# The third gate/up piece is split into the sums' buffer, the first unit's h turns round in two parts, and split weights are stored later

## The chip, the core and the metric

One core of a Trainium2 chip runs the program. The metric is the device time of one execution in microseconds, the median of several runs; the program is the same in every run. The names of the engines are those of the profile: PE (TensorE, with PEld for its weight loads), DVE (VectorE), ACT (ScalarE), POOL (GpSimd) and SP (SyncE, which issues nearly all DMAs).

## What is computed

```python
xn = layernorm(x)                                   # x: 2048 x 576
q, k, v = split(xn @ wqkv)                          # 32 heads of 18
s = softmax(q @ k.T / sqrt(18)) @ v @ wo            # per head, 2048 x 2048 scores
g = silu(((xn @ w_gate) * (xn @ w_up)) @ w_down)    # w_gate, w_up: 576 x 4608
out = x + s * g
```

Both branches read the same normalised x. All inputs and the output are fp32.

## The kernel before, in words

**Precision.** A matmul operand of the projections and of the gated branch is split into a high part (a rounding copy by ACT) and a low part (value minus high part, by POOL), and the products high x high, low x high and high x low are summed in PSUM. "Splitting" a piece of weights below means these copies and differences.

**The gated branch** is cut into 72 units: 4 chunks of 512 rows (c) times 18 column blocks (q) of 256 columns. A unit has two *pieces* n = 2u and 2u+1, each 128 columns of w_up and w_gate together. Up columns stand on partitions 0 to 63 and gate columns on 64 to 127, so PE runs two streams side by side, each on one half of its rows: the *upper* stream does the "up" of a piece in 27 matmuls, the other its "gate" in 27 (L678). When an up is done, ACT copies its sum out (us, L683). When a gate is done, DVE multiplies the two (L690, h), ACT takes the high part (L693) and POOL the low part (L694), both into hs. The product with w_down (L720) needs h in both halves of the rows, so two DMAs carry hs crosswise into hx (the *turning round*, L710): one for each half of the rows, and the two streams then add hs and hx terms for four row blocks. The sums (acc) are gathered by DVE (L746, L748).

**The streams** run in this order: both pieces of unit u+1, then the down products of unit u. Beside them PE computes scores for the row maxima (pa, L596, reduced by DVE in L598), the scores again in transposed form (pb, L628, with exp by ACT in L630, two PSUM banks), and in *visits* of 28 matmuls (56 records of the trace) the products of the probabilities with v (L639).

**Weights in chunk 0.** A piece is loaded raw into wraw (two buffers, L116) and split into wgu, 128 x 18 x 128, two buffers: ACT's three copies in L193, POOL's three differences in L194. Piece n+2 goes into the buffer of piece n. The split piece is stored in DRAM as swg (L199, 1152 KB) so that chunks 1 to 3 can load it ready split (L185). w_down goes the same way through draw, wd and swd. `g_get` queues a piece's splitting as *chores*; `chore` runs one of them when the planner finds room.

**What sets the order.** Each engine runs its instructions in the order in which the code records them. A planner written in Python (`order`) keeps a clock for each of the two streams and a table of engines, PSUM banks and transfers with fixed costs, and records whatever can go next. So a changed cost or a changed call moves rows on all engines for the rest of the program. All of SP's DMAs stand in one queue, and an SP instruction that waits holds up the ones behind it.

**The buffer of the sums.** `accp` has one buffer, 128 x 4 x 576 of fp32. The sums of row chunks 0 and 2 live in it from the first down product of unit 0 on; before that it is unused.

Of the kernel before, what the change touches and what calls it, by code (L numbers as in the profile page):

```python
# [20 lines left out]
FT = mybir.dt.float32  # L21
# [19 lines left out]
def kernel(  # L41
# [10 lines left out]
    nc = tc.nc  # L52
# [109 lines left out]
    graw, gw, draw, dw = {}, {}, {}, {}  # L162
# [6 lines left out]
    def g_get(n):  # L169
# [13 lines left out]
        w = gw[n] = g_tile()  # L183
# [13 lines left out]
        def end():  # L197
            gdone.add(n)
            nc.sync.dma_start(swg[f], w.bitcast(FT))  # L199
            g_load(n + 2)  # L200

        chores.extend([(piece, (b,)) for b in (0, 3, 6)] + [(end, ())])

# [374 lines left out]
    with ExitStack() as mid:  # L578
# [106 lines left out]
        def gate_end(n, ps):  # L685
            u, j = divmod(n, 2)
            if j == 0:
                hs[u] = gp.tile([128, 2, 2, 512], FR, name="hs", bufs=2)
            h32 = us.pop(n)
            nc.vector.tensor_tensor(h32, ps, h32, op=OP.mult)  # L690
            g_get(n + 2)
            hj = hs[u][:, j]
            nc.scalar.activation(hj[:, 0, :], h32, AF.Copy)  # L693
            nc.gpsimd.tensor_tensor(hj[:, 1, :], h32, hj[:, 0, :].bitcast(FT), op=OP.subtract)  # L694
            if u == 0 and j or u == len(units) - 1:
                turn_round(u, j)
# [3 lines left out]
        def turn_round(u, j):  # L700

            if u == len(units) - 1:
                if j == 0:
                    hx[u] = accp.tile([128, 2, 2, 512], FR, name="hxl", tag="acc")
                js = slice(j, j + 1)
            else:
                hx[u] = gp.tile([128, 2, 2, 512], FR, name="hx", bufs=1)
                js = slice(0, 2)
            for r in range(2):
                nc.sync.dma_start(hx[u][half[r], js].bitcast(FT), hs[u][half[1 - r], js].bitcast(FT))  # L710
# [137 lines left out]
        def stream(r):  # L848

            for u in range(len(units) + 1):  # L850
                for n in (2 * u, 2 * u + 1):
# [4 lines left out]
                    for k in range(len(TERMS)):  # L856
                        def work(n=n, k=k, box=box, c=c, q=q):
                            if k == 0:
                                box.append(gu_start(r, n))
                            gu_op(r, n, box[0], k)  # L860
# [250 lines left out]
        def order():  # L1111
            nonlocal na, nb
            load_v(0)
            feeds = [stream(0), stream(1)]
            heads.extend(next(f) for f in feeds)
            wait = None
            while any(heads) or na < TOTAL or nb < TOTAL or due:
# [35 lines left out]
                elif op is not None:  # L1153
# [8 lines left out]
                    if end:  # L1162
# [11 lines left out]
                        else:  # L1174
# [20 lines left out]
        heads, stuck, parts, loaded, stacks = [], [False], {}, {}, []  # L1195
# [118 lines left out]
```

## Time and profile before

| | us |
|---|---|
| median of 3 runs (lowest, highest) | 2570.12 (2569.12, 2572.28) |
| the profiled execution, its time | 2571.43 |
| its span, first to last instruction | 2569.4 |
| PE busy | 2547.8 (99%) |
| ACT busy | 1467.1 (57%) |
| DVE busy | 1933.2 (75%) |
| DMA queue of SP, share of the 16 engines over the span | 68.6% |

PE's first matmul of the gated branch (L678) starts at 195.1 us, and its last matmul of the down products (L720) ends at 2501.1; between them is the *main phase*. PE is reported as busy when either half of it works, so a stretch in which only one stream runs still reads as 10 of 10 us busy; the number of matmuls in a stretch tells the difference. The granted clock is 1.00 in the windows shown below.

### The profile page before, as it was taken

How to read it: one execution, taken by the hardware profiler on the slowest of the kernel's cores; microseconds unless marked ns; L12 is line 12 of the kernel's file. 1: busy time of each engine (PE TensorE's matmuls, PEld its weight loads, DVE VectorE, ACT ScalarE, POOL GpSimd, SP SyncE). 2: the span in 40 equal slices, each digit the busy share in tenths (PEclk: the TensorE clock that was granted, in tenths of full speed). 3: DMA queues.
4: the chain of work that ended last, by engine and by line, in shares of the span. 5: the costliest groups of instructions: out<-in, count | busy, mean ns of one | idle time of the engine just before them, and what ended most of it. 6: DMA issues, size and time to landing. Idle time of an engine off the chain costs nothing.

```text
span 2569.4 us, 59203 instructions
## 1 busy us (share of the span) xinstructions
PE 2547.8 (99%) x24360; PEld 2111.1 (82%) x24360; DVE 1933.2 (75%) x3377; ACT 1467.1 (57%) x2688; POOL 594.8 (23%) x663
## 2 busy tenths in 40 slices
PE   8999999999999999999999999999999999999999
PEld 7899888878878888877888888777888877888878
DVE  6208778777778898777778888777888887778437
ACT  5222666666756665555665665555665655556651
POOL 3214434434421111111111111111111111111125
PEclk9999999999999999999999999999999999999999
DMA  7799988888886666665686656665686666654567
GB/s 243 235 284 278 263 226 225 232 225 220 221 206 186 176 182 177 175 179 155 179 197 173 179 175 184 176 170 154 179 204 166 180 184 176 175 174 146 159 189 248
DMA packets 195898, 504.58 MB, mean 196 GB/s; under 512 B 58112, under 2 KB 116352, under 8 KB 156588
## 3 DMA queue, kind: packets, MB, share of 16 engines
q1 hardware_dynamic: 185676, 489.05, 68.6%
q0 software_dynamic: 9952, 11.74, 1.7%
q8 instruction: 192, 3.15, 0.6%
q14 instruction: 78, 0.64, 0.1%
HBM read 312.21 MB, written 107.61 MB: 163 GB/s over the span
## 4 chain that ended last, share of the span: by engine, by line
PE 95%; DMA 3%; DVE 1%; SPq 0%; ACT 0%; issue 0%; POOL 0%; ACTq 0%; DVEq 0%
PE pg L678 34%; PE pg L639 18%; PE pg L720 16%; PE pa L596 12%; PE pb L628 8%; PE pg L402 2%; PE pa L348 2%; PE pb L348 2%; PE pg L1244 1%; DMA hx<-hs 1%; PE pb L1244 1%; PE pa L1244 1%; DMA sqk<-hl 0%; DMA ring<-sqk 0%; DMA xc<-sx 0%; DMA o<-sot 0%
## 5 line engine op out<-in xcount | busy, mean ns | idle before, releaser
L598 DVE TENSOR_REDUCE mx<-pa 128x1 f32<-128x512 f32 x2048 | 1367.1, 686 | 223.6 <-PE pa L596 104.8
L630 ACT ACTIVATE pt<-pb 128x512 f32<-128x512 f32 x2048 | 1161.9, 598 | 534.8 <-PE pb L628 465.5
L678 PE MATMUL pg<-xc,wgu 64*128 64x512 f32 x7776 | 1366.1, 388 | 0.7 <-DMA xc<-sx 0.5
L678 PEld LDWEIGHTS pg<-xc,wgu 64*128 64x128 f32 x7776 | 1051.7, 184 | 41.6 <-DMA xc<-sx 1.2
L628 PE MATMUL pb<-pair,ring 64*128 64x512 f32 x1997 | 777.4, 395 | 1.5 <-DMA ring<-sqk 1.5
L596 PE MATMUL pa<-pair,ring 64*128 64x512 f32 x2006 | 776.9, 393 | 1.8 <-DVE mx L598 1.8
L720 PE MATMUL pg<-wd,hs 64*128 64x288 f32 x3408 | 523.4, 292 | 0.0
L720 PE MATMUL pg<-wd,hx 64*128 64x288 f32 x3408 | 515.2, 292 | 2.4 <-DMA hx<-hs 2.4
L694 POOL TENSOR_TENSOR hs<-us,hs 128x512 fp32r<-128x512 f32 x144 | 186.2, 1293 | 1320.3 <-ACT hs L693 1285.6
L720 PEld LDWEIGHTS pg<-wd,hs 64*128 64x128 f32 x3408 | 459.8, 185 | 4.0 <-DVE acc L748 0.2
L720 PEld LDWEIGHTS pg<-wd,hx 64*128 64x128 f32 x3408 | 453.4, 185 | 6.5 <-DMA hx<-hs 3.0
L639 PE MATMUL pg<-pt,vt 128*32 128x512 f32 x4096 | 454.8, 594 | 0.7 <-DVE acc L748 0.6
L596 PEld LDWEIGHTS pa<-pair,ring 64*128 64x128 f32 x2006 | 364.3, 184 | 69.8 <-issue 52.8
L628 PEld LDWEIGHTS pb<-pair,ring 64*128 64x128 f32 x1997 | 362.5, 184 | 8.7 <-issue 1.9
L639 PEld LDWEIGHTS pg<-pt,vt 128*32 128x32 f32 x4096 | 125.5, 110 | 284.0 <-issue 278.9
L748 DVE TENSOR_TENSOR acc<-acc,pg 128x288 f32<-128x288 f32 x544 | 233.0, 443 | 22.4 <-PE pg L720 21.4
L645 DVE TENSOR_TENSOR oc<-oc,pg 128x512 f32<-128x512 f32 x69 | 47.1, 683 | 220.4 <-PE pg L639 213.7
L693 ACT ACTIVATE hs<-us 128x512 fp32r<-128x512 f32 x144 | 91.0, 632 | 151.0 <-DVE us L690 149.7
L194 POOL TENSOR_TENSOR wgu<-wraw,wgu 128x384 fp32r<-128x384 f32 x108 | 108.6, 1017 | 97.1 <-ACT wgu L193 84.6
L643 ACT ACTIVATE oc<-pg 128x512 f32<-128x512 f32 x32 | 19.2, 598 | 185.0 <-PE pg L639 179.0
L690 DVE TENSOR_TENSOR us<-pg,us 128x512 f32<-128x512 f32 x144 | 98.2, 682 | 26.9 <-PE pg L678 15.7
L618 POOL DMA_DIRECT2D pair<-mt x128 | 77.8, 613 | 166.4 <-DVE mt L613 162.3
(141 smaller groups left out, 1359.0 us busy)
## 6 DMA issues: line engine op xcount, KB each, us to landing
wgu<-swg SPq DMA_DIRECT2D x102, 1152.0 KB
hx<-hs SPq DMA_DIRECT2D x142, 512.0 KB
wd<-swd SPq DMA_DIRECT2D x50, 1152.0 KB
swg<-wgu SPq DMA_DIRECT2D x36, 1152.0 KB
pair<-sqk SPq DMA_DIRECT2D x192, 144.0 KB
ring<-sqk SPq DMA_DIRECT2D x384, 72.0 KB
swd<-wd SPq DMA_DIRECT2D x18, 1152.0 KB
sqk<-hl SPq DMA_DIRECT2D x32, 512.0 KB
```

The costliest lines, as they stand in the source:

```text
L194: nc.gpsimd.tensor_tensor(w[:, 9 + b:12 + b, :], raw[:, b:b + 3, :], w[:, b:b + 3, :].bitcast(FT), op=OP.subtract)
L348: nc.tensor.matmul(p, wq[b, a], xcs[c][:, e, :], start=n == 0, stop=n == len(PAIRS) - 1)
L596: nc.tensor.matmul(p, q[rows, t * 128:(t + 1) * 128], k[rows, c * 512:(c + 1) * 512], start=True, stop=True)
L598: nc.vector.tensor_reduce(mx[h][:, t, c:c + 1], p, axis=AX.X, op=OP.max)
L628: nc.tensor.matmul(p, k[rows, t * 128:(t + 1) * 128], q[rows, c * 512:(c + 1) * 512], start=True, stop=True)
L630: nc.scalar.activation(pt[t, c], p, AF.Exp, scale=scale)
L639: nc.tensor.matmul(p[32 * c:32 * c + 32, :], vt[h // 2][:, t, 6 * (h % 2):6 * (h % 2) + 32], pt[t, c], start=t == ts[0], stop=t == ts[-1])
L678: nc.tensor.matmul(ps, gw[n][half[r], a, :], xg[i][half[r], e, :], start=k == 0, stop=k == len(TERMS) - 1)
L690: nc.vector.tensor_tensor(h32, ps, h32, op=OP.mult)
L694: nc.gpsimd.tensor_tensor(hj[:, 1, :], h32, hj[:, 0, :].bitcast(FT), op=OP.subtract)
L720: nc.tensor.matmul(ps[:, 0:HALF], (hx if k else hs)[u][half[r], j, a, s * 128:(s + 1) * 128], dw[u][half[r], k, j, e, :], start=n == 0, st ...
L748: nc.vector.tensor_tensor(a, a, ps[:, 0:HALF], op=OP.add)
```

## The change

1. Piece 2 is split into a tile of the sums' buffer, called wg2, as soon as the planner starts, and not into piece 0's buffer after gate 0. The later pieces follow at other places: piece 3 takes piece 0's buffer after gate 0, piece 4 takes piece 1's after gate 1, gate 2 calls for nothing, and from gate 3 on piece n+2 follows gate n as before.
2. The store of a split piece to swg is taken out of the end of its splitting and goes where the gate stream starts on that piece. The next raw load, which stood behind the store, now stands alone.
3. Unit 0 turns its h round in two parts, one after each of its two gates, two DMAs of 256 KB each time.
4. The planner's table is told of the new places: when a piece counts as loaded, and 0.524 in place of 1.05 for unit 0's turning.

```diff
@@ -159,7 +159,7 @@
         c, q = units[u]
         return NF2 - 1 - q if c % 2 else q
 
-    graw, gw, draw, dw = {}, {}, {}, {}
+    graw, gw, draw, dw, unsaved = {}, {}, {}, {}, {}
     gdone, ddone = set(), set()
 
     def g_load(n):
@@ -180,7 +180,7 @@
             gw[n] = gw[n - 2]
             gdone.add(n)
             return
-        w = gw[n] = g_tile()
+        w = gw[n] = accp.tile([128, 18, 128], FR, name="wg2", tag="acc") if n == 2 else g_tile()
         if n >= 2 * NF2:
             nc.sync.dma_start(w.bitcast(FT), swg[f])
             gdone.add(n)
@@ -196,10 +196,18 @@
 
         def end():
             gdone.add(n)
+            unsaved[n] = f, w
+            g_load(n + 2)
+
+        chores.extend([(piece, (b,)) for b in (0, 3, 6)] + [(end, ())])
+
+    def g_save(n):
+        if n in unsaved:
+            f, w = unsaved.pop(n)
             nc.sync.dma_start(swg[f], w.bitcast(FT))
-            g_load(n + 2)
-
-        chores.extend([(piece, (b,)) for b in (0, 3, 6)] + [(end, ())])
+
+    def g_after(n):
+        return {0: 3, 1: 4, 2: None}.get(n, n + 2)
 
     def d_load(n):
         if n < NF2:
@@ -688,11 +696,12 @@
                 hs[u] = gp.tile([128, 2, 2, 512], FR, name="hs", bufs=2)
             h32 = us.pop(n)
             nc.vector.tensor_tensor(h32, ps, h32, op=OP.mult)
-            g_get(n + 2)
+            if g_after(n):
+                g_get(g_after(n))
             hj = hs[u][:, j]
             nc.scalar.activation(hj[:, 0, :], h32, AF.Copy)
             nc.gpsimd.tensor_tensor(hj[:, 1, :], h32, hj[:, 0, :].bitcast(FT), op=OP.subtract)
-            if u == 0 and j or u == len(units) - 1:
+            if u in (0, len(units) - 1):
                 turn_round(u, j)
 
         hx = {}
@@ -704,8 +713,9 @@
                     hx[u] = accp.tile([128, 2, 2, 512], FR, name="hxl", tag="acc")
                 js = slice(j, j + 1)
             else:
-                hx[u] = gp.tile([128, 2, 2, 512], FR, name="hx", bufs=1)
-                js = slice(0, 2)
+                if u or j == 0:
+                    hx[u] = gp.tile([128, 2, 2, 512], FR, name="hx", bufs=1)
+                js = slice(0, 2) if u else slice(j, j + 1)
             for r in range(2):
                 nc.sync.dma_start(hx[u][half[r], js].bitcast(FT), hs[u][half[1 - r], js].bitcast(FT))
 
@@ -857,6 +867,8 @@
                         def work(n=n, k=k, box=box, c=c, q=q):
                             if k == 0:
                                 box.append(gu_start(r, n))
+                                if r:
+                                    g_save(n)
                             gu_op(r, n, box[0], k)
                             if q == NF2 - 1 and n % 2 and k % 3 == 2 and c < NCH - 1:
                                 x_block(c + 1, k // 3, (64 * r,))
@@ -1111,6 +1123,7 @@
         def order():
             nonlocal na, nb
             load_v(0)
+            g_get(2)
             feeds = [stream(0), stream(1)]
             heads.extend(next(f) for f in feeds)
             wait = None
@@ -1175,11 +1188,12 @@
                             gated[n] = done
                             fin = engine("ACT", done + 0.05, 0.535)
                             fin = engine("POOL", fin + 0.05, 1.29)
-                            loaded[n] = moved(done - 0.4, 1.18) if (n // 2 + 1) % NF2 else 0.0
+                            if n != 2:
+                                loaded[g_after(n) - 2] = moved(done - 0.4, 1.18) if (n // 2 + 1) % NF2 else 0.0
                             if n // 2 == len(units) - 1:
                                 there["h", n // 2] = moved(fin, 0.524)
-                            elif n == 1:
-                                there["h", 0] = moved(fin, 1.05)
+                            elif n < 2:
+                                there["h", 0] = moved(fin, 0.524)
                             for _ in range(2):
                                 hot = n + 2 >= 2 * NF2 and n % (2 * NF2) in (34, 35, 0) and n + 2 < 2 * len(units)
                                 for want in stacks:
@@ -1192,7 +1206,7 @@
                 else:
                     clk[r] = max(clk[r] + 0.05, min(clk[1 - r] + 0.01, clk[r] + 0.3))
 
-        heads, stuck, parts, loaded, stacks = [], [False], {}, {}, []
+        heads, stuck, parts, loaded, stacks = [], [False], {}, {0: 0.0}, []
         order()
 
 
```

The built program's order shows it at three places.

SP's queue at the start of the main phase, before; `swg<-wgu` are stores of split pieces, `wraw` raw loads, the number behind a name its buffer (wgu_1762 is piece 1, wgu_2030 piece 2):

```order
112 L410 DMA sv_80<-vo2_427 128x608
113 L410 DMA sv_80<-vo0_423 128x608
114 L410 DMA sv_80<-vo4_1166 128x608
115 L410 DMA sv_80<-vo3_1164 128x608
116 L199 DMA swg_78<-wgu_1762 128x2304
117 L116 DMA wraw_1902<-in_B_w_up_dram 64x9x128
118 L116 DMA wraw_1902<-in_B_w_gate_dram 64x9x128
119 L584 DMA vt_1917<-sv_80 128x16x38
120 L199 DMA swg_78<-wgu_2030 128x2304
```

and with the change (wgu_1311 is piece 0, wraw_1900 the raw piece 3, wraw_1936 the raw piece 4):

```order
111 L418 DMA sv_80<-vo2_427 128x608
112 L418 DMA sv_80<-vo0_423 128x608
113 L418 DMA sv_80<-vo4_1166 128x608
114 L418 DMA sv_80<-vo3_1164 128x608
115 L116 DMA wraw_1900<-in_B_w_up_dram 64x9x128
116 L116 DMA wraw_1900<-in_B_w_gate_dram 64x9x128
117 L592 DMA vt_1915<-sv_80 128x16x38
118 L116 DMA wraw_1936<-in_B_w_up_dram 64x9x128
119 L116 DMA wraw_1936<-in_B_w_gate_dram 64x9x128
120 L207 DMA swg_78<-wgu_1311 128x2304
```

Piece 0's store, issued long before the main phase until now, stands behind two raw loads and the load of vt; piece 1's comes two rows later.

ACT with the semaphores that each row waits for (DMAHW are those of SP's DMAs), the copies out of up 0, up 1 and up 2 and the splits between them, before:

```order
118 L683 ACTIVATE us<-pg 128x512 [waits PE_49]
119 L693 ACTIVATE hs<-us 128x512 [waits DVE_49]
120 L193 ACTIVATE wgu<-wraw 128x384 [waits DMAHW5_49,PE_49,Pool_49]
121 L193 ACTIVATE wgu<-wraw 128x384 x2
122 L683 ACTIVATE us<-pg 128x512 [waits PE_49]
```

and with the change:

```order
121 L691 ACTIVATE us<-pg 128x512 [waits PE_49]
122 L702 ACTIVATE hs<-us 128x512 [waits DVE_49]
123 L193 ACTIVATE wgu<-wraw 128x384 [waits DMAHW4_49,DMAHW0_49,DMAHW7_49,PE_49,Pool_49]
124 L193 ACTIVATE wgu<-wraw 128x384 x2
125 L691 ACTIVATE us<-pg 128x512 [waits PE_49]
```

The split after gate 0, of piece 2 before and of piece 3 now, waits for three DMAs: the two raw loads of piece 3, and the store of piece 0 that reads the buffer which the split overwrites.

SP's queue in a later unit of chunk 0 (unit 5, pieces 10 and 11), before:

```order
164 L116 DMA wraw_3680<-in_B_w_up_dram 64x9x128
165 L116 DMA wraw_3680<-in_B_w_gate_dram 64x9x128
166 L710 DMA hx_3755<-hs_3381 64x2048 x2
167 L232 DMA swd_79<-wd_3754 128x2304
168 L124 DMA draw_3790<-in_B_w_down_dram 64x2x288 x4
169 L245 DMA ring_1154<-sqk_76 18x1024 x6
170 L245 DMA pair1_1153<-sqk_76 18x2048 x3
171 L199 DMA swg_78<-wgu_3905 128x2304
```

and with the change:

```order
163 L116 DMA wraw_3679<-in_B_w_up_dram 64x9x128
164 L116 DMA wraw_3679<-in_B_w_gate_dram 64x9x128
165 L720 DMA hx_3746<-hs_3368 64x2048 x2
166 L207 DMA swg_78<-wgu_3370 128x2304
167 L240 DMA swd_79<-wd_3745 128x2304
168 L124 DMA draw_3779<-in_B_w_down_dram 64x2x288 x4
169 L253 DMA ring_1154<-sqk_76 18x1024 x6
170 L207 DMA swg_78<-wgu_3547 128x2304
```

The store of the unit's first piece (wgu_3370) now stands right behind the turning of h, and that of the second (wgu_3547) behind the store of w_down's block, four raw loads of the next one and the ring's loads.

More of the change, by code (lines that the diff above doesn't have):

```diff
@@ L198, in end @@
             gdone.add(n)
-            nc.sync.dma_start(swg[f], w.bitcast(FT))
+            unsaved[n] = f, w
             g_load(n + 2)
         chores.extend([(piece, (b,)) for b in (0, 3, 6)] + [(end, ())])
+    def g_save(n):
+        if n in unsaved:
+            f, w = unsaved.pop(n)
+            nc.sync.dma_start(swg[f], w.bitcast(FT))
+    def g_after(n):
+        return {0: 3, 1: 4, 2: None}.get(n, n + 2)
     def d_load(n):
```

## The prediction

> **What bounds the kernel now.** I read the page's chain of waits first, then who waits for whom in chunk 0 (330 to 700 us), then the windows and the timelines of ACT and SP at the start of the main phase. The page's chain and the groups of the two ACT steps that matter here:
>
> ```profile
> PE 95%; DMA 3%; DVE 1%; SPq 0%; ACT 0%; issue 0%; POOL 0%; ACTq 0%; DVEq 0%
> L630 ACT ACTIVATE pt<-pb 128x512 f32<-128x512 f32 x2048 | 1161.9, 598 | 534.8 <-PE pb L628 465.5
> ```
>
> PE's waits from 330 to 700 us (row: who, for whom, us in total, times, longest), and from all groups the row of the splits:
>
> ```profile
> PE pg L678 <- DVE acc L748: 0.2, 1, 0.2
> ...
> PEld pa L596 <- DVE oc L645: 0.8, 1, 0.8
> ```
>
> ```profile
> L193 ACT ACTIVATE wgu<-wraw 128x384 fp32r<-128x384 f32 x108 | 54.1, 520 | 2.0 <-DMA wraw<-in_B_w_gate_dram 2.0
> ```
>
> PE sets the end. In chunk 0 it waits for almost nothing, and ACT stands still before all 108 split copies for 2.0 us together. What can be won lies at the start, and it is little; what can be lost is a PE that never waits now. The windows (us, busy and count by engine, clock, DMA share, GB/s):
>
> ```profile
> 200.00:210.00 10.00, 10.00 (x85) 9.55 (x82) 8.90 (x14) 3.07 (x6) 3.54 (x4) 1.00 1.03 328
> 210.00:220.00 10.00, 10.00 (x72) 8.14 (x71) 8.78 (x14) 2.52 (x5) 4.89 (x5) 1.00 1.17 224
> 270.00:280.00 10.00, 7.57 (x81) 6.85 (x79) 6.04 (x10) 5.01 (x10) 3.45 (x4) 1.00 0.98 249
> 380.00:390.00 10.00, 10.00 (x95) 10.00 (x94) 8.44 (x18) 7.72 (x14) 2.87 (x2) 1.00 1.03 247
> ```
>
> From 210 to 220 us only 72 matmuls run where 85 ran before: one half of PE is empty for a while. From 270 to 280 PE is idle for 2.43 us. The DMA engines are full (share about 1.0) in all four.
>
> **The change, part by part.** *Piece 2 earlier.* ACT's timeline around pieces 0 to 3 (start, duration, what), with POOL's part of a split:
>
> ```profile
> 201.52 0.60 ACT L683 ACTIVATE us<-pg 128x512 f32<-128x512 f32 x1 [5.92 <-PE pg L678]
> 205.75 0.63 ACT L693 ACTIVATE hs<-us 128x512 fp32r<-128x512 f32 x1 [3.63 <-DVE us L690]
> 206.29 1.34 ACT L193 ACTIVATE wgu<-wraw 128x384 fp32r<-128x384 f32 x3
> 208.80 0.60 ACT L683 ACTIVATE us<-pg 128x512 f32<-128x512 f32 x1 [1.18 <-PE pg L678]
> ...
> 218.72 0.60 ACT L683 ACTIVATE us<-pg 128x512 f32<-128x512 f32 x1 [3.20 <-PE pg L678]
> ```
>
> ```profile
> 207.72 2.96 POOL L194 TENSOR_TENSOR wgu<-wraw,wgu 128x384 fp32r<-128x384 f32 x3
> ```
>
> ```profile
> 195.09 0.49 PE L678 MATMUL pg<-xc,wgu 64*128 64x512 f32 x1
> ...
> 204.06 0.91 PE pg L678 x8
> ```
>
> The phase begins at 195.1. Eight matmuls of two streams take 0.91 us, so a stream needs 0.228 us for each and 6.2 us for the 27 of an up. Up 1 ends at about 208.4, up 2 at 218.3, so up 2 began near 212.1, 17.0 us into the phase. In the order before, the upper stream has 60 matmuls ahead of it (13.7 us); in the new order it has 59 (13.5 us) and no gap. Gain: 17.0 - 13.5, about 3.4 us. The split itself, 1.34 us of ACT and 2.96 of POOL, moves to where ACT is idle for 5.92 us and costs nothing; without that cover it would delay the first us copy by at most 1.3.
>
> *Stores later.* Piece n+2 overwrites piece n's buffer, so its split must wait until the store of piece n has landed. Until now that store was issued at least a gate earlier; now it is issued when gate n begins, and ACT, which runs in order, stands at the split until the DMA is through. Queued behind it on ACT are the copy of the next up and the exps, which give PE its banks back. The price is the landing time of the store against the length of a gate.
>
> SP's rows at the start, and the only turnings whose landing the chain of waits shows:
>
> ```profile
> 199.08 2.50 SPq L410 DMA_DIRECT2D sv<-vo  x4
> 207.57 0.38 SPq L584 DMA_DIRECT2D vt<-sv  x1
> 202.94 0.66 SPq L116 DMA_DIRECT2D wraw<-in_B_w_up_dram  x1
> 203.65 1.37 SPq L116 DMA_DIRECT2D wraw<-in_B_w_gate_dram  x1
> ```
>
> ```profile
> 239.12 8.29 DMA hx<-hs
> 266.87 11.50 DMA hx<-hs
> ```
>
> *The first store.* In the new queue piece 0's store follows the load of vt, which waits for the stores of sv and cannot go before 207.6, and a raw load of 0.66 + 1.37 us: it goes at 209.7. Two DMAs of this time landed 8.29 and 11.50 us after their issue with the queue as full as here; alone, 1152 KB (1.18 MB) at the 247 GB/s of 380 to 390 us take 4.8 us. Taking 8.3, it lands at 218.0. ACT reaches the split of piece 3 at 206.3 as before, and waits. Piece 3 is ready one copy (0.52) and POOL's 2.96 later, at 221.5. The new order has 91 matmuls ahead of up 3 on the upper stream, 20.8 us, so PE wants it at 195.1 + 20.8 = 215.9 and waits 5.6 us. With the gain: **+2.2 us** for the start; with 4.8 us of landing -1.3, with 11.5 +5.4.
>
> *A unit of chunk 0.* A gate takes 27 matmuls and, by the new order, 8 to 13 scores of its own half: 36 x 0.228 = 8.2 us. DVE's product and ACT's high part follow (these two groups, DVE and ACT):
>
> ```profile
> L690 DVE TENSOR_TENSOR us<-pg,us 128x512 f32<-128x512 f32 x144 | 98.2, 682 | 26.9 <-PE pg L678 15.7 <-PE pb L628 10.4
> L693 ACT ACTIVATE hs<-us 128x512 fp32r<-128x512 f32 x144 | 91.0, 632 | 151.0 <-DVE us L690 149.7 <-DMA hx<-hs 0.6 <-DMA ring<-sqk 0.6
> ```
>
> With 0.5 for the hand-overs, ACT asks for the buffer 10.0 us after the gate began, or 16.1 when a visit falls inside the gate:
>
> ```profile
> 299.36 6.15 PE pg L639 x56
> 329.49 6.14 PE pg L639 x56
> ```
>
> The first piece's store stands right behind the turning, which is issued about when its gate begins. With the 8.29 us row it lands at 8.3 + 4.8 = 13.1, so ACT stands still for 3.1 us; if the queue were empty, (1.05 + 1.18) MB at 247 GB/s give 9.0 and no wait. The second piece's store has the first one, swd, four raw blocks and itself behind that: 1.18 + 0.59 + 1.18 MB and some ring loads, 3.17 MB, 12.8 us later, at 21.8 to 25.9. Its gate begins 8.2 us after the first, so it lands 13.6 to 17.7 us into it: 3.6 to 7.7 us too late without a visit, 0 to 1.6 with one.
>
> PE feels a standing ACT only when both exp banks are full: one exp per 1.13 us (2048 in the phase of 2306 us) and two banks, so I let 1.5 us of each stall go free (between one exp, 0.6, and two intervals, 2.3). By the new order the visit lies in the second gate in units 4 to 8, in the first in units 9 to 13, in neither in 1 to 3 and 14 to 17. So the first piece stalls PE for 0 to 1.6 us in 12 units, 0 to 19; the second, in the four last without a visit, for 2.1 to about 4.6 us (the first stall has pushed the gate back by 1.6), 8 to 18; with a visit hardly. Which end is nearer, the later windows tell:
>
> ```profile
> 340.00:350.00 10.00, 10.00 (x127) 9.92 (x125) 10.00 (x20) 8.35 (x17) 3.06 (x3) 1.00 0.40 94
> 350.00:360.00 10.00, 10.00 (x92) 9.96 (x89) 8.95 (x15) 7.82 (x16) 4.93 (x5) 1.00 0.91 241
> ...
> 410.00:420.00 10.00, 10.00 (x102) 9.96 (x100) 9.08 (x17) 8.64 (x17) 5.80 (x5) 1.00 0.68 150
> ```
>
> The queue is neither empty there nor always as full as at 240, so I take the middle: **+9.6 and +13 us**. In units 1 to 3 no exps wait yet; left to the range.
>
> *The end of chunk 0.* Chunk 1's x blocks are loaded there and gate PE:
>
> ```profile
> 736.55 8.06 DMA xc<-sx
> 744.63 11.52 DMA ring<-sqk
> ```
>
> Piece 35's store now stands among them, ahead of 17 of the 20 loads: 0 to 4.8 us, taken as **+2.4**.
>
> *The turning of unit 0* in halves moves the same bytes with two more DMA issues; the second part goes after gate 1 as the whole did, so what the down products wait for last is half as large and no later: nothing. *The planner's new costs* reshuffle the rest, with the same number of matmuls. Laid out on the two halves at their durations, without any wait, the whole new order is 1.5 us shorter than the old one, less than the 3.4 of its start, so I count nothing more; chunks 1 to 3 have no stores of pieces.
>
> Sum: 2.2 + 9.6 + 13 + 2.4 = **+27.2 us**. The profiled span of 2569.4 becomes 2596.6; its execution's time was 2.0 above the span, and the median lies 1.3 below that time, so the median goes from 2570.1 to **2597.3 us**. The bounds add up to -1.3 + 0 + 8 + 0 = +7 and 5.4 + 19 + 18 + 4.8 = +47, 2577 to 2617: the forecast's own range.
>
> **Rivals.** *The stores land in time.* If a turning and a store behind it take less than the 10.0 us of a gate, ACT never stands, and the gain of 3.4 us stays, with up to 2.4 more if the turning behind PE's idle 2.43 us (270 to 280) comes sooner because no store waits for POOL ahead of it: 2564.3 to 2566.7. For it speaks that ACT waits 2.0 us in all today; against it the 8.29 and 11.50 us rows, which leave no room for 1.18 MB more. By the Trainium skill, "DMA: Bandwidth & Descriptors", section "Anatomy of one DMA — SWDGE (gpsimd) path", a DMA takes 2.0 us and its bytes at 436 GB/s; worked out from that, an estimate, turning and store need 7.1 us and the second store 7.3 more, and neither would be late. The windows' 224 to 328 GB/s at a share of 1.0 disagree with that rate here. Chance 0.14.
>
> *Only the start pays.* Once the queue has caught up, the exp banks swallow what is left of the stalls: +2.2, 2572.3. For it: 1.5 of 3.1 us are free already. Against: the second piece's store is late even with an empty queue. Chance 0.14.
>
> *The queue stays as full as at 267 us.* Each store lands 11.50 + 4.8 = 16.3 us after the turning, the first piece costs 4.8 us of PE in 12 units: 57 and more, 2630. This decides if later stores also hold the raw loads and turnings behind them back. The windows from 340 to 420 us do not look so full. Chance 0.08.
>
> **Chances and range.** The forecast has 0.64, the rivals 0.14, 0.14 and 0.08. A change under 0.2% (5.1 us) is about what cannot be told from none here. Faster by more: half of the first rival and a little, 0.08. Within: the rest of it and most of the second, 0.16. Slower: 0.76. The range 2567 to 2622 leaves out about half of the first rival and the third.
>
> **What would show it.** Piece 2: the second and third us copies of the upper stream 6 to 7 us apart. The stores: L193's idle time must rise from 2.0 to some 50 us or more, with the store swg<-wgu as releaser; PE's waits for the exps (pb, L630) must appear in chunk 0 and be absent in chunks 1 to 3; POOL's differences shift with ACT. If L193 still waits for some 2 us, the forecast falls whatever the time is. If the idle time is there but PE does not wait, the free 1.5 us was too little. If PE waits for other things (the sums' buffer, the ring), the place was wrong.

## The result and the profile after

| | before | after |
|---|---|---|
| median of 4 runs each, us (lowest, highest) | 2570.04 (2569.12, 2572.28) | 2610.07 (2605.55, 2612.99) |
| the profiled execution, its time | 2571.43 | 2605.55 |
| its span | 2569.4 | 2603.6 |

The ratio is 1.0147, with a 95% interval of 1.0135 to 1.0159: the change makes the kernel slower by 35 to 41 us (38 at the ratio). The forecast was slower, 2597.3, in a range of 2567 to 2622. The profiled execution of after is the fastest of its four runs, 4.5 us below their median; that of before lay 1.4 above. So the two traces differ by 34.1 us and the medians by 40.0.

The chain of waits of after by engine, the group of the split copies, and PE's waits from 195 to 800 us (who, for whom, us in total, times, longest):

```profile
PE 89%; DMA 5%; DVE 2%; SPq 1%; issue 1%; POOL 1%; ACT 1%; ACTq 0%; POOLq 0%; DVEq 0%
```

```profile
L193 ACT ACTIVATE wgu<-wraw 128x384 fp32r<-128x384 f32 x105 | 53.5, 522 | 45.9 <-DMA swg<-wgu 31.5 <-issue 6.7 <-DMA ring<-sqk 4.5
```

```profile
PE pb L636 <- ACT pt L638: 14.5, 8, 3.4
PE pb L636 <- DMA pair<-mt: 4.9, 1, 4.9
PE pa L604 <- DVE mx L606: 4.5, 1, 4.5
PE pg L686 <- DMA xc<-sx: 1.6, 2, 1.3
```

PE's share of the chain fell from 95 to 89%. ACT stood still ahead of the split copies for 45.9 us instead of 2.0, mostly until a store of a split piece (swg<-wgu) had landed. PE now waits for the exps (pt) in chunk 0, eight times and 14.5 us in all. From 800 to 2400 us it waits for none of them again; the largest row of PE there is this one:

```profile
PE pa L604 <- DVE mx L606: 1.5, 3, 0.5
```

One stall in full, in unit 6: the store on the chain from 365 to 390 us, then ACT's timeline, then PE's wait in the same window.

```profile
370.38 9.95 DMA swg<-wgu
```

```profile
376.03 1.07 ACT L638 ACTIVATE pt<-pb 128x512 f32<-128x512 f32 x2
380.43 0.52 ACT L193 ACTIVATE wgu<-wraw 128x384 fp32r<-128x384 f32 x1 [3.34 <-DMA swg<-wgu]
380.86 0.58 ACT L638 ACTIVATE pt<-pb 128x512 f32<-128x512 f32 x1
```

```profile
PE pb L636 <- ACT pt L638: 2.3, 1, 2.3
```

The store is issued at 370.38 and lands at 380.33. ACT has done its last exp at 377.1, stands before the split for 3.34 us, and the next exp starts at 380.86. Of the 3.34 us, PE loses 2.3.

Where the 34 us are lost is seen from the start of each up (its first matmul on PE, counted in the program's order from the first matmul of the phase; worked out from PE's records of both traces):

```
up                   2     3     4     6     8    10    12    16    26    28    32    36    40   end of phase
before, us        16.7  24.6  38.4  61.9  88.7 119.7 151.6 215.6 376.0 407.9 478.4 542.7 609.3
after - before    -3.2  +2.5  +3.8  +4.7  +9.8 +15.2 +17.0 +20.0 +19.8 +20.9 +25.8 +29.5 +31.5  +34.0
```

Unit u begins with up 2u. Units 2 to 7 lose 16 us, units 8 to 13 no more than 1, units 14 to 17 some 9, the turn to chunk 1 another 2.

Not all of the 34 us are waits. From 190 to 810 us PE stands idle for 26.6 us, 21.2 more than before. A second part is the granted clock. In the main phase of before it is 1.00 throughout; in the trace of after it falls to 0.50 in five stretches, one of 6.8 us from 216.7 and four of 3.4 us from 267.9, 312.3, 660.5 and 776.5. The window of the first one (us, busy and count by engine, clock, DMA share, GB/s), and the same kind of matmul in it and behind it:

```profile
210.00:220.00 10.00, 5.55 (x44) 4.66 (x42) 4.59 (x7) 2.66 (x6) 4.14 (x4) 0.84 0.92 312
```

```profile
222.02 0.62 PE L686 MATMUL pg<-xc,wgu 64*128 64x512 f32 x1
225.06 0.39 PE L686 MATMUL pg<-xc,wgu 64*128 64x512 f32 x1
```

PE works for 18.6 us of these 20.5 at half the clock, which costs some 9 us (an estimate: half of 18.6). Each stretch begins within a wait of PE or at most 1.5 us behind one. The four waits of 2.7 us and more (2.75 to 4.91) were all followed by one, and so was the turn to chunk 1, where the longest of several short waits is 1.35; two waits of 2.3 us, at 379 and 714, were not, and neither was that of 2.2 in before. That the waits bring the lower clock is read from this order in time; no run here changes the clock alone.

### The profile page after: what moved, and what is told of

It reads as the page before. It is cut to its first block, busy times and chain, and to the rows that moved or that the text cites. A ratio compares the mean times of both kernels' runs of the same rounds, so it can differ in the third digit from the quotient of the medians.

```text
span 2603.6 us, 59193 instructions
## 1 busy us (share of the span) xinstructions
PE 2559.3 (98%) x24360; PEld 2117.1 (81%) x24360; DVE 1930.9 (74%) x3377; ACT 1461.8 (56%) x2688; POOL 592.9 (23%) x663
## 4 chain that ended last, share of the span: by engine, by line
PE 89%; DMA 5%; DVE 2%; SPq 1%; issue 1%; POOL 1%; ACT 1%; ACTq 0%; POOLq 0%; DVEq 0%
PE pg L686 31%; PE pg L647 17%; PE pg L730 14%; PE pa L604 10%; PE pb L636 8%; DMA swg<-wgu 3%; PE pg L410 2%; PE pa L356 2%; PE pb L356 2%; PE pg L1258 1%; DVE mx L606 1%; DMA o<-sot 1%; PE pa L1258 1%; PE pb L1258 1%; DMA sqk<-hl 0%
## 5 line engine op out<-in xcount | busy, mean ns | idle before, releaser
L636 PE MATMUL pb<-pair,ring 64*128 64x512 f32 x2013 | 785.5, 396 | 19.6 <-ACT pt L638 14.5
L730 PE MATMUL pg<-wd,hx 64*128 64x288 f32 x3408 | 509.4, 292 | 0.0
L698 DVE TENSOR_TENSOR us<-pg,us 128x512 f32<-128x512 f32 x144 | 98.4, 684 | 24.7 <-PE pg L686 14.1
```

The lines of the kernel that those rows point to most:

```text
L636: nc.tensor.matmul(p, k[rows, t * 128:(t + 1) * 128], q[rows, c * 512:(c + 1) * 512], start=True, stop=True)
L730: nc.tensor.matmul(ps[:, 0:HALF], (hx if k else hs)[u][half[r], j, a, s * 128:(s + 1) * 128], dw[u][half[r], k, j, e, :], start=n == 0, st ...
```

## The experiments

Each experiment is timed against the kernel before on the same chip. Three theories go in. *Standing ACT*: the late store of the buffer's earlier piece holds the next split, and ACT, in order, holds the exps and us copies behind it. *New order*: the order of TensorE's work, the halved turning and piece 2's place cost the time. *Traffic*: late stores only crowd the DMA queue, and others wait for that. (A ratio's interval is given behind it; where two runs are compared by their ratios, both intervals count.)

**Stores early again, all else as changed.**

```diff
         def end():
             gdone.add(n)
-            unsaved[n] = f, w
+            nc.sync.dma_start(swg[f], w.bitcast(FT))
             g_load(n + 2)
```

> The change with its third part undone: the stores of split weights go at the end of the split again; piece 2 in the sums' buffer, the halved turning and the new order of the tensor engine stay. Standing ACT (a late store of a buffer's earlier piece holds the next split, and ACT stands in order before it): 2566 to 2572 us, idle time before the split copies (L193) back to 2 to 5 us. New order (the order, the halves or piece 2 cost the time, the place of the stores nothing): 2600 to 2610 us. Traffic (late stores collide in the DMA queue with turnings, ring and x loads, and PE waits for those): as standing ACT, 2566 to 2572 us.

Measured: 2580.85 against 2571.48, ratio 1.0039 (1.0025 to 1.0053). So 28 of the 38 us come with the late stores, but 10 do not, and neither figure expected held. PE's waits from 195 to 800 us in this run:

```profile
PE pb L636 <- DMA pair<-mt: 5.4, 1, 5.4
PE pa L604 <- DVE mx L606: 2.9, 1, 2.9
PE pg L730 <- DMA hx<-hs: 1.7, 1, 1.7
```

The waits for exps are all but gone (0.2 us); three others stay, and all come before 290 us. They are taken up below. The splits still stand for 11.9 us, more than the 2 to 5 expected, now with a raw load as releaser (wraw<-in_B_w_gate_dram). The clock is at 0.50 for 10.2 us, which is up to half of what stays.

**The late stores alone, in the kernel before.** The four places of the store as in the change, nothing else; TensorE's order is that of before.

```diff
         def end():
             gdone.add(n)
-            nc.sync.dma_start(swg[f], w.bitcast(FT))
+            unsaved[n] = f, w
             g_load(n + 2)
...
                             if k == 0:
                                 box.append(gu_start(r, n))
+                                if r:
+                                    g_save(n)
```

> The kernel before with the late stores alone: the store of piece n goes when gate n begins, everything else and the order of the tensor engine as before. Standing ACT: 2592 to 2606 us, the split copies' idle time 35 to 60 us with the store swg<-wgu as what ended it. New order: 2568 to 2572 us. Traffic: 2592 to 2606 us too, but with PE waiting for loads and turnings, not for the exps and the row maxima.

Measured: 2603.63, ratio 1.0119 (1.0104 to 1.0134), +31 us. The group of splits, PE's waits from 195 to 800 us, and the longest stall on ACT's timeline:

```profile
L193 ACT ACTIVATE wgu<-wraw 128x384 fp32r<-128x384 f32 x108 | 54.2, 520 | 50.7 <-DMA swg<-wgu 31.0 <-issue 12.3 <-PE pg L683 5.6
```

```profile
PE pb L633 <- ACT pt L635: 18.7, 5, 9.7
```

```profile
284.23 1.35 ACT L193 ACTIVATE wgu<-wraw 128x384 fp32r<-128x384 f32 x3 [11.62 <-DMA swg<-wgu]
```

The late stores make the loss by themselves, with the old order too, and PE waits for the exps above all: 18.7 us, against 4.4 for loads (xc, pair and ring). The longest stretch at half the clock, 13.7 us, begins within the longest wait, of 9.7 us.

**The same late traffic, but no split that waits for it.** The stores of pieces 0 to 33 read the x tile. Chunks 1 to 3 then load pieces 34 and 35 over and over (a second edit, not shown), so this kernel does not compute the formula; the DMAs are as many and as large.

```diff
     def g_save(n):
         if n in unsaved:
             f, w = unsaved.pop(n)
-            nc.sync.dma_start(swg[f], w.bitcast(FT))
+            if n < 34:
+                src = xg[0].rearrange("p a b -> p (a b)")[:, 0:2304]
+                nc.sync.dma_start(swg[f].rearrange("p a b -> p (a b)"), src.bitcast(FT))
+            else:
+                nc.sync.dma_start(swg[f], w.bitcast(FT))
```

> The change, but the late stores of pieces 0 to 33 read as many bytes from the x tile in place of the split weights, at the same place in the queue, so that no split has to wait for one; in chunks 1 to 3 the reloads take pieces 34 and 35 over and over. The number and size of all DMAs are the same; what chunks 1 to 3 compute is not the reference's. Standing ACT: 2566 to 2575 us, the split copies' idle time below 8 us. Traffic: 2598 to 2612 us, as the change, since every byte still moves late. New order: 2600 to 2610 us.

Measured: 2577.36, ratio 1.0021 (1.0011 to 1.0031). That is 2.4 us above what *standing ACT* had said and far below *traffic*. The split copies:

```profile
L193 ACT ACTIVATE wgu<-wraw 128x384 fp32r<-128x384 f32 x105 | 53.4, 522 | 3.4 <-DMA wraw<-in_B_w_gate_dram 3.4
```

The bytes of the late stores, at the same place in the queue, cost nothing that can be seen: this run is no slower than the one with early stores. What costs is that the split must wait for them. *Traffic* falls. *New order* falls as the main cause, but holds for the 5 to 10 us that stay.

**Half of each store late.** The high half of a piece is stored at the end of the split, the low half when the gate begins.

```diff
+            nc.sync.dma_start(swg[f][:, 0:9, :], w[:, 0:9, :].bitcast(FT))
             unsaved[n] = f, w
...
-            nc.sync.dma_start(swg[f], w.bitcast(FT))
+            nc.sync.dma_start(swg[f][:, 9:18, :], w[:, 9:18, :].bitcast(FT))
```

> The change, with the high halves of a piece (columns 0 to 8) stored at the end of the split and only the low halves when the gate begins: half the bytes are late. Standing ACT: the late half lands 2 to 3 us sooner, and what stands before the three copies is shorter by that in each unit, so less than half of the loss is left: 2576 to 2590 us, idle time before the copies 10 to 30 us. Traffic: half the late bytes, half the loss, about 2588 us or more. New order: 2600 to 2610 us.

Measured: 2587.77, ratio 1.0059 (1.0044 to 1.0074). Against early stores, half of the bytes late cost some 5 us (1.0059 less 1.0039; by the intervals 0 to 10) where all of them cost 28. The time fits both bounds, 2576 to 2590 for *standing ACT* and about 2588 for *traffic*, and decides nothing alone.

```profile
L193 ACT ACTIVATE wgu<-wraw 128x384 fp32r<-128x384 f32 x105 | 53.4, 522 | 23.1 <-DMA swg<-wgu 22.9
```

The idle time halves, and PE's waits for exps fall to a fifth (from 14.5 to 2.9 us): a stall of ACT costs PE only what is left after its banks' slack.

**Late only in units 8 to 13.**

```diff
-            unsaved[n] = f, w
+            if 16 <= n < 28:
+                unsaved[n] = f, w
+            else:
+                nc.sync.dma_start(swg[f], w.bitcast(FT))
```

> The change with the late stores in units 8 to 13 alone, where the visit lies in the first gate; in all other units the stores go at the end of the split. If a late store costs only where no visit covers its landing (the trace of the change grows by 15 us in units 2 to 7, by nothing in 8 to 13, by 9 in 14 to 17): as with all stores early, 2578 to 2584 us. If every late store costs alike (29 us over 17 units): 2588 to 2594 us.

Measured: 2583.31, ratio 1.0048 (1.0034 to 1.0062), against 1.0039 with all stores early. So these twelve late stores cost some 2 us together, which cannot be told from nothing; PE still waits for exps three times, 3.3 us in all. (In unit 8 the visit still lies in the second gate; from unit 9 on it lies in the first.) No group row names a store any more:

```profile
L193 ACT ACTIVATE wgu<-wraw 128x384 fp32r<-128x384 f32 x105 | 53.4, 522 | 17.4 <-PE pg L689 7.9 <-PE pa L607 4.4 <-issue 3.7
```

**Each store one gate earlier.**

```diff
                                 if r:
                                     g_save(n)
+                                    g_save(n + 1)
```

> The change with each late store issued one gate earlier (piece n+1 is stored when gate n begins; at the start piece 0 and 1 together). If the loss is the landing time of a store against the length of a gate: one gate more, 8 us or above, covers most landings, 2581 to 2587 us and less than 10 us of idle time at the splits with a store as what ended it. If stores anywhere behind the split cost (order of the queue, traffic): 2595 us or more.

Measured: 2595.40, ratio 1.0091 (1.0078 to 1.0105): half of the loss by the late stores is left. 2581 to 2587 us had been expected, and the time lies in the range that had been set for *traffic*; since the run with the x tile rules that out, the cause must be looked for in when the stores are issued. SP's timeline around the start of unit 4, first of the change, then of this run:

```profile
296.56 1.22 SPq L720 DMA_DIRECT2D hx<-hs  x2
...
300.01 5.61 SPq L207 DMA_DIRECT2D swg<-wgu  x1
...
313.41 0.34 SPq L207 DMA_DIRECT2D swg<-wgu  x1
```

```profile
290.31 1.22 SPq L720 DMA_DIRECT2D hx<-hs  x2
...
292.71 7.72 SPq L207 DMA_DIRECT2D swg<-wgu  x2
```

The odd piece's store, 13.4 us behind the even one in the change, now stands next to it. The even one hardly moves: it still stands behind the turning (hx<-hs) on SP, 2.4 us in place of 3.4. The idle time at the splits falls from 45.9 to 25.9 us, and PE's waits for exps from 14.5 to 9.5. This fits a price of landing time against the time until the split, but the place in the program did not give the time of issue; SP's order did.

**What stays with early stores: piece 2, the halves, the order.** Two runs start from the kernel before and do one part alone, with the old order of TensorE. A third does both.

```diff
-        w = gw[n] = g_tile()
+        w = gw[n] = accp.tile([128, 18, 128], FR, name="wg2", tag="acc") if n == 2 else g_tile()
...
-            g_get(n + 2)
+            if g_after(n):
+                g_get(g_after(n))
...
             load_v(0)
+            g_get(2)
```

> The kernel before with piece 2 split early into the sums' buffer, and nothing else: the turning whole, the stores at the end of a split, and the very order of TensorE's instructions as before (the planner's costs are left as they were). In the run with early stores 9 us of loss stayed, 3.3 of them behind up 2, where piece 3's raw block landed at 213.2 us behind the store of piece 1. If the new order and the halved turning make the rest: up 2 begins 3 us sooner, up 3 as before, 2568 to 2574 us. If piece 2's own place makes the loss (its buffer, its store, the raw blocks behind it): 2577 to 2583 us.

Measured for piece 2 alone: 2575.87, ratio 1.0019 (1.0010 to 1.0028), about 5 us slower (2.6 to 7.2). That lies between the two ranges expected, so neither held.

```diff
-            if u == 0 and j or u == len(units) - 1:
+            if u in (0, len(units) - 1):
...
-                hx[u] = gp.tile([128, 2, 2, 512], FR, name="hx", bufs=1)
-                js = slice(0, 2)
+                if u or j == 0:
+                    hx[u] = gp.tile([128, 2, 2, 512], FR, name="hx", bufs=1)
+                js = slice(0, 2) if u else slice(j, j + 1)
```

> The kernel before with the first unit's turning in two parts, and nothing else (order of TensorE's instructions as before). If the second part lands no later than the whole did: 2568 to 2573 us. If the halves cost the 3.4 us that the run with early stores lost between up 3 and up 4, where a half turning landed 10.7 us after its issue: 2573 to 2576 us.

Measured for the halves alone: 2571.27, ratio 1.0005 (0.9995 to 1.0014): nothing that can be told from zero.

Both together, with the old order (the two diffs above in one kernel):

> The kernel before with piece 2 early and the halved turning, stores at the end of the split, and the old order of TensorE's instructions: the run with early stores (2580.9) but for the order. If the new order costs what piece 2 alone (2575.9) and the halves alone (2571.3) leave over, some 4.5 us, most of it PE's wait for the first head's row pair (pair<-mt, landed 9.1 us after its issue): 2574 to 2578 us. If it is the two edits together and the order is innocent: 2579 to 2583 us.

Measured: 2575.65, ratio 1.0015 (1.0005 to 1.0024). With the new order the same edits had given 1.0039, so the new order costs about 6 us (2 to 11). Its sign in the trace is the wait for pair<-mt, the row maxima of the first head on their way into the pair tile: 5.4 us with the new order, and not among PE's waits in this run with the old one:

```profile
PE pa L604 <- DVE mx L606: 4.1, 2, 3.4
PE pg L730 <- DMA hx<-hs: 2.8, 1, 2.8
PE pb L636 <- DMA ring<-sqk: 1.6, 1, 1.6
```

In TensorE's list the first exp score stands at place 591 of the phase before and 592 now, but the last score of the first head's maxima went from place 460 to 485. That is 24 matmuls less in between, some 2.7 us at eight in 0.91 us, for a DMA that takes this long (chain of the run with early stores):

```profile
258.15 9.13 DMA pair<-mt
```

Piece 2 alone shows what it does on the chain from 205 to 220 us:

```profile
214.20 1.35 ACT wgu L193 x3
215.55 0.49 ACT us L691
...
216.07 0.69 DVE us L698
216.76 0.61 DVE mx L606
```

Piece 3 is now asked for after gate 0, and its raw block is not there until 213 to 214 us (the chain of the run with both edits has its DMA):

```profile
203.39 9.67 DMA wraw<-in_B_w_gate_dram
```

ACT stands at its split, and the us copy of up 1, gate 1's product and DVE's row maxima queue up behind. Up 2 does not begin sooner at all (16.7 us into the phase, as before): the old order has it no earlier in its list, so the gain of 3.2 us at up 2 comes only with the new order. Up 3 begins 5.3 us later than before (29.9 in place of 24.6).

**Two repairs of the start, with the old order.** First piece 3's raw load ahead of the store of piece 1:

```diff
+            if n == 1:
+                g_load(n + 2)
             nc.sync.dma_start(swg[f], w.bitcast(FT))
-            g_load(n + 2)
+            if n != 1:
+                g_load(n + 2)
```

> As the run with piece 2 early and the old order, and in addition the raw load of piece 3 is issued ahead of the store of piece 1 instead of behind it. If the start's gain was lost to that raw load: piece 3's raw block lands near 207 us, up 3 begins 3 to 4 us sooner than before, and some of it stays to the end: 2566 to 2570 us. If not: like the run without it, within 1 us.

Measured: 2574.46, ratio 1.0012 (1.0003 to 1.0021). The split of piece 3 begins at 209.1 in place of 214.2, and up 3 begins 24.7 us into the phase, 5.2 sooner than with piece 2 alone, but no sooner than before (24.6). At up 4 the run is 3.3 us behind before. Neither bound was met: 2566 to 2570 was missed, and the run lies 1.4 us below the one without the edit, where 1 had been allowed, though that is within the scatter. Then also the splits of pieces 3 and 4 behind the us copies of up 1 and 2, and piece 4's raw load ahead of the store in front of it:

```diff
             nc.scalar.activation(us[n], ps, AF.Copy)
+            if n in (1, 2):
+                g_get(n + 2)
...
-            if g_after(n):
-                g_get(g_after(n))
+            if n > 2:
+                g_get(n + 2)
```

> As the run with piece 3's raw load first, but pieces 3 and 4 are asked for behind the us copies of up 1 and up 2 on ScalarE instead of at the ends of gates 0 and 1, and piece 4's raw load too goes ahead of the store in front of it. If the start's gain is lost because a split that waits (for its raw block or for a store) stands in front of the us copy of the next up: that copy is back near 207 us, up 3 begins 3 us or more sooner than before, 2566 to 2569 us. If the full DMA queue takes the gain in another place (the turning of unit 0 lands later): 2570 to 2574 us.

Measured: 2575.16, ratio 1.0013 (1.0004 to 1.0022); neither bound held. Its ACT timeline, and the turning on its chain:

```profile
207.96 0.60 ACT L694 ACTIVATE us<-pg 128x512 f32<-128x512 f32 x1 [2.42 <-PE pg L689]
209.91 1.35 ACT L193 ACTIVATE wgu<-wraw 128x384 fp32r<-128x384 f32 x3 [1.35 <-DMA wraw<-in_B_w_gate_dram]
```

```profile
216.47 12.88 DMA hx<-hs
```

The us copy is in its old place again, with no split in front of it, and up 3 begins as before. Now the turning of unit 0 takes 12.9 us to land, and PE waits 5.1 us for turnings (2.4 before). SP has issued the stores of pieces 2 and 3 and the raw blocks of pieces 4 and 5 just ahead of it; that they delay it is argued, not tested.

**All repairs in the changed kernel.** Late stores for pieces 1 to 3 alone, the splits of 3 and 4 behind the us copies, and 9 us in place of 6 in the planner from the first head's maxima to its row pair.

```diff
-            unsaved[n] = f, w
+            if n in (1, 2, 3):
+                unsaved[n] = f, w
+            else:
+                nc.sync.dma_start(swg[f], w.bitcast(FT))
...
                                     g_save(n)
+                                    if n == 2:
+                                        g_save(3)
...
-                rows_done[h] = engine("DVE", 0.0, 0.85) + ROWS
+                rows_done[h] = engine("DVE", 0.0, 0.85) + (9.0 if h == 0 else ROWS)
```

> The change (piece 2 early, halved turning, new order) with three things put right that the runs before point at: late stores only for pieces 1, 2 and 3 (3 behind the second part of the turning), pieces 3 and 4 asked for behind the us copies of up 1 and up 2, and the planner reckoning with 9 us instead of 6 from the first head's row maxima to its row pair (first exp-score of that head at place 649 of TensorE's list instead of 592). If late stores, splits in front of the us copies and the row pair are the whole loss: up 3 begins 3 us or more sooner than before, no wait for pair<-mt, no store as what ended idle time at the splits, 2564 to 2569 us. If the full queue of the first 100 us takes the gain elsewhere again (a turning, a raw block): 2571 to 2578 us, and the wait has a DMA's name.

Measured: 2571.94 against 2571.76, ratio 1.0001 (0.9992 to 1.0010): the whole loss is gone, and nothing is won that can be told from zero; the 2564 to 2569 us expected were missed. In the one profiled execution, the fastest of eleven, up 3 begins 3.9 us sooner than before, the span is 3.1 us shorter, and the clock is 1.00 in the whole main phase. PE's waits from 195 to 800 us:

```profile
PE pg L650 <- DVE acc L763: 0.7, 2, 0.5
PE pb L639 <- ACT pt L641: 0.4, 1, 0.4
PE pg L735 <- DVE acc L761: 0.4, 1, 0.4
```

No kernel here beats the kernel before by more than its runs scatter.

## Why the prediction was right in sign and too small

**Standing ACT: right.** L193's idle time was to rise from 2.0 to some 50 us with the store as releaser; it rose to 45.9. PE's waits for the exps were to appear in chunk 0 alone; they did. The run with the x tile as source shows that it is this wait and not the traffic. The late stores cost 28 us with the new order (1.0147 less 1.0039) and 31 with the old one. The terms for them added up to 25.0 (9.6 + 13 + 2.4), to which the start's 5.6 us of waiting belongs too. Of the loss in the trace, a part is not waiting but the lower clock behind the waits (some 9 us by the estimate above); the prediction had no term for it.

**Their place in the units: half right.** The run with early stores has the very order of PE's matmuls that the change has, so the difference of these two traces is the late stores alone (worked out as the table above):

```
up                            2     3     4     6     8    10    12    16    26    28    32    36    40   end of phase
after - early stores, us    0.0  +2.4  +0.3  +0.8  +0.9  +6.3  +8.4 +11.1 +11.7 +12.6 +17.4 +20.2 +24.5  +24.3
```

Units 9 to 13 were forecast to lose nothing, and 8 to 13 lost 1.5. Units 14 to 17 were to lose 16.2 (4 x 0.8 + 13) and lost 7.6. Units 2 to 7 were to lose 4.8 (6 x 0.8) and lost 10.8, nearly all of it in units 4 to 6. The chain of after shows eight stores from issue to landing:

```profile
207.94 7.11 DMA swg<-wgu
253.64 8.13 DMA swg<-wgu
283.05 8.47 DMA swg<-wgu
300.01 6.68 DMA swg<-wgu
334.17 9.60 DMA swg<-wgu
370.38 9.95 DMA swg<-wgu
650.32 7.62 DMA swg<-wgu
703.52 11.65 DMA swg<-wgu
```

Counted along SP's stores, these are pieces 0, 5, 7, 8, 10, 12, 29 and 32. The rows of 300.01 and 334.17 end before the store is through: the splits behind them begin at 310.16 and 345.24, and by the trace's semaphore updates the last parts of these two stores land at 310.08 and 345.17, so they took 10.1 and 11.0 us. (The groups put these two stalls to "issue".) In units 2 and 3, which have no visit, it is the second piece; in units 4 to 6, where a visit lies in the second gate, the first; in 14 the second, in 16 the first. So the rule of the visits held, but for unit 16. Two sizes failed. The first pieces were priced at 0.8 us, the middle between an empty queue and the one of 240 us: in units 4 to 6 a store takes 10.0 to 11.0 us, one stall of 3.34 us cost 2.3 (so 1.0 was free, not 1.5), and the lower clock behind a wait came on top. In units 14 to 17 the middle was too full a queue. The prediction also charged first pieces in units 1 to 3, where by its own words no exps wait yet; with the late stores PE lost 0.6 us in units 2 and 3.

**The first store at the start: size right, place wrong.** +2.2 was forecast at up 3, +2.5 came. It did not last: at up 4 the run with early stores stands at +3.5 too, against +3.8 with the change. And PE did not wait there for piece 3. ACT's and DVE's timelines of after:

```profile
215.24 1.35 ACT L193 ACTIVATE wgu<-wraw 128x384 fp32r<-128x384 f32 x3 [9.06 <-DMA swg<-wgu]
216.49 0.57 ACT L691 ACTIVATE us<-pg 128x512 f32<-128x512 f32 x1
```

```profile
217.10 0.69 DVE L698 TENSOR_TENSOR us<-pg,us 128x512 f32<-128x512 f32 x1 [4.83 <-ACT us L691]
217.71 1.28 DVE L606 TENSOR_REDUCE mx<-pa 128x1 f32<-128x512 f32 x2
```

The us copy of up 1 stood behind the split on ACT, gate 1's product behind that on DVE, the row maxima behind the product; PE's 4.5 us are put down to the row maxima. The prediction named the us copy as queued behind the split, but priced the arrival of the weights. The sign it had set, the us copies of up 1 and up 2 six to seven us apart, all but came (216.49 and 222.32, 5.8 us), but proves nothing: the stall delays both.

**Piece 2 earlier, -3.4: wrong.** Up 2 does begin 3.2 us sooner, but by the new order: with the old one piece 2's early split moves nothing there. And by up 3 the gain is gone, with stores early (+0.1) as with stores late. The step that failed is "ACT reaches the split of piece 3 at 206.3 as before". At 206.3 ACT had split piece 2, whose raw block was there; with piece 2 done early, the split at this place is piece 3's, whose raw block stands behind a store on SP and lands at 213.1 in the run with both edits. Asked for a gate early, it holds everything behind it on ACT. Alone it costs 5 us.

**The planner's order, nothing: wrong.** Counting its matmuls on both halves, 1.5 us shorter, says nothing of what it leaves for a DMA in between. It takes some 3 us away from the first head's row pair, and by the runs costs about 6.

**The halves, nothing: right** (1.0005).

**The end of chunk 0, +2.4: right in kind, too small.** From up 36 to up 40 the difference to before grows by 2.0, but the run with early stores falls by 2.3 there, so the late stores cost 4.3. PE waits 1.6 us for the x blocks (xc<-sx), and the last stretch at half the clock lies there. The 2.5 us that come after up 40 belong to the new order: with early stores it is +7.0 at up 40 and +9.7 at the end, with the old order (the run with both edits) +5.3 and +5.1.

**The sum.** Forecast for the profiled execution +27.2, measured +34.1. Late stores 28 to 31 against 30.6 forecast with the start; the other edits +10 where -3.4 was forecast; the parts overlap in the start, so they do not simply add. That the stores' sum fits is luck in part: too little in units 4 to 6, too much in 14 to 17, and a clock that nobody had reckoned with. The other 5.9 us between the medians are the places of the two profiled executions, 1.4 above the median before and 4.5 below it after.

**The rivals.** *Stores land in time*, with the rule of the Trainium skill's page "DMA: Bandwidth & Descriptors" behind it (section "Anatomy of one DMA — SWDGE (gpsimd) path"), falls: the eight stores above take 7.1 to 11.7 us each, where the estimate from its figures had 7.1 for a turning and a store together. The page's fit is for one DMA that GpSimd issues; these are SP's, in a queue that others share. *Only the start pays* falls. *The queue stays as full as at 267 us* priced a first piece at 4.8 us; unit 4 lost 5.4, units 5 and 6 lost 2.1 and 2.7, and units 8 to 13 next to nothing, so it falls as well.

## What to carry to other kernels

A store that reads a buffer is part of that buffer's next write. Moving the store later, even to "when nobody needs the queue", moves the wait to the engine that overwrites the buffer, and what counts is what else stands in that engine's queue: here exps and copies that free PE's banks. The same holds for asking early: work should be put into an in-order queue when its input is there, not when its output buffer is.

A wait of the main engine can cost more than its length. Read the granted clock behind each wait, and not only the waits.

A new order of the main engine's work must be priced by the gaps it leaves for DMAs between producer and consumer, not by its count of instructions.

## What the runs showed of the hardware

The issue of a store of 1152 KB held SP for 0.34 us at one place and for 5.05 at another, with early stores at the start:

```profile
207.01 0.38 SPq L592 DMA_DIRECT2D vt<-sv  x1
207.44 5.05 SPq L199 DMA_DIRECT2D swg<-wg  x1
212.54 0.61 SPq L116 DMA_DIRECT2D wraw<-in_B_w_up_dram  x1
```

The raw loads behind it went 5 us later for that. So a store can cost twice, in the landing and in the issue of all that stands behind on SP; the prediction had reckoned only with the landing. A full queue alone does not explain it: the DMA share was 1.22 during the long issue, and 1.11 from 313 to 314 us of after, where the issue of a store took 0.34.

In the main phase the granted clock was either 1.00 or 0.50, and the stretches at 0.50 lasted 3.4 us or whole multiples of it, up to 13.7.

And variants that differ in the first 100 us alone scatter more than the kernel before: piece 2 with halves and the old order ran in 2570.7 to 2581.1 us over 10 executions. The clock has a part in it: its mean was 0.999 in the fastest and 0.997 in the slowest, which is some 5 us of the 10.4 (0.002 of 2571, an estimate). The rest is open.
